# Five runs of attention products per pair of heads in place of seven, and maxima turned by an ordinary product

## The chip, the cores and the metric

The kernel runs on one core of a Trainium2 chip. The metric is the device time of one execution in microseconds (us). Three runs of the kernel before gave a median of 999.97 us (999.01 to 1001.33). The engines are named as the profile names them: PE is the matrix engine, PEld its loads of the stationary operand, DVE VectorE, ACT ScalarE, POOL GpSimd, SP SyncE, which issues nearly all DMAs.

## The reference

Two independent parts share one output of 2048 rows, 576 columns each.

```python
def _A_ref(x, wq, wk, wv, wo, beta):     # x: 1 x 2048 x 576, 32 heads of 18, 4 segments of 512 rows
    q, k, v = (heads and segments of) x @ wq, x @ wk, x @ wv
    phi = lambda t: jnp.where(t > 0, t + 1.0, jnp.exp(t))
    for s in range(4):
        logits = jnp.einsum("bhqd,bhkd->bhqk", qs, ks) * scale + mask      # causal inside the segment
        p = _softmax(logits, axis=-1)
        a_dot = jnp.einsum("bhqk,bhkd->bhqd", p, vs)
        a_mem = (phi(qs) @ M) / (phi(qs) @ z + 1e-6)
        o = g * a_mem + (1.0 - g) * a_dot
        M, z = M + phi(ks).T @ vs, z + sum(phi(ks))
    return concat(o) @ wo

def _B_ref(x, dft_seq_re, dft_seq_im, dft_hid_re, dft_hid_im):
    a = jnp.einsum("bsd,ed->bse", x, dft_hid_re)
    b = jnp.einsum("bsd,ed->bse", x, dft_hid_im)
    return jnp.einsum("ts,bse->bte", dft_seq_re, a) - jnp.einsum("ts,bse->bte", dft_seq_im, b)
```

The output holds A's result in columns 0 to 575 and B's in columns 576 to 1151.

## The kernel before

Float32 precision is kept by splitting operands into a high and a low part, so that a dense product of the reference is three products on PE (high by low, high by high, low by high).

**Stages.** Up to about 218 us the kernel projects q, k and v, builds the memory part, and writes q, k and v as split 16-bit pieces to DRAM. From there to about 930 us two streams of work share PE. The last 66 us are the product with `wo` (from L1013).

**The dense stream** is a generator `dense()`: all of part B. Per half (real, imaginary) it makes 16 tiles of `hidden` (L619, products in L628 to L633) and 16 tiles of `sequence` (L641, products through `product` in L583). Each of its products has a 128x128 stationary block and 288 moving columns, in f32r. Its results go to PSUM tiles `d`, of which there are three; they are freed by ACT (L634, L651) or by DVE (the subtractions of L635, shown at a line of the queue that runs late work, and of L653).

**The attention stream** is a generator `attention()` (L921). It goes through 68 periods `p`; 32 groups `G` of four heads make 64 pairs of heads, one of them even and one odd, and a pair's steps are spread over five periods (`F_LAG`, `T_LAG`, `V_LAG` = 2, 3, 4). All its products are on 16-bit operands. The scores of a head (512 queries by 512 keys, lower triangle) are made in three pieces, `ROWS`: kind 0 is row block 3 (one product of 512 columns), kind 1 row blocks 0 and 2 (products of 128 and 384), kind 2 row block 1 (256).

- `s_fill` (even head, L753): scores (L744) whose only use is the row minimum of their negative, which DVE takes (L750) into `NEGM`. The product's bank is free when the minimum is done.
- `f_fill` (odd head, L759): the same products and minima; then ACT takes the exponentials (`f_exp`, L773) from the same bank, `f_split_hi` and `f_split_lo` split the result, and `f_turn` transposes it by a DMA.
- `t_fill` (even head, L807): scores transposed (L818, L821, L826, L827), with the maxima coming in as extra rows of the product; ACT takes the exponentials (L830, L831).
- `pv` (L847): the products with v (L862, L863), many and short; `pv_out` (L865) normalizes on DVE.
- `maxima` (L791): POOL splits the minima of a group into three 16-bit pieces, in 24 columns of a 128x128 tile `MB`, zeros elsewhere. `maxima_transpose` (L799) turns that tile on PE against the identity, into columns 384 on of a bank, ACT copies 24 rows out (L803), and two DMAs put them beside the queries.

**Order of the work.** The schedule is written by hand. Each period has eight slots, and at each `yield` of `attention()` the main loop (L994 to L1001) adds as many dense products as make the two streams keep step by the costs in `SLOTS`. So the attention products of one slot, or of several where no dense products fall between them, form a run on PE, with dense products on both sides. Each engine works in program order. The operations that are put off with `later` are issued at the start of a later slot.

**PSUM banks** (`bank`, L564): the scores `s` alternate between two banks, the transposed scores `t` between two others, which kind 0 of `f_fill` shares; the second of a period's `t` banks also takes the turned maxima. One bank is for `pv`.

Of the kernel before, what the change touches and what calls it, by code (L numbers as in the profile page):

```python
# [15 lines left out]
BF16 = mybir.dt.bfloat16  # L16
# [24 lines left out]
def infini_attention_and_fnet(ctx: ExitStack, tc: tile.TileContext, xT, wqk, w8, wv, wo, beta, xtT, cT, hT, out):  # L41
    nc = tc.nc
    act, dve, pool, pe = nc.scalar, nc.vector, nc.gpsimd, nc.tensor
# [25 lines left out]
    ident16 = const.tile([P, P], BF16, name="ident16")  # L69
# [18 lines left out]
    def later(n, fn, *a):  # L88
        due.setdefault(clock[0] + n, []).append((fn, a))
# [112 lines left out]
    for i in range(2):  # L202
        kn.append(tuple(sk.tile([P, D], F32R, name=f"kn{n}{i}") for n in "hl"))
        t = sk.tile([P, 2, H, 19], F32R, name=f"vn{i}")
# [3 lines left out]
    for i in range(3):  # L208
        t = sb.tile([P, H, 55], BF16, name=f"vs{i}")
# [253 lines left out]
    def stacks(p_, i):  # L463
        qs_bufs.append(p_.tile([P, 4, L], BF16, name=f"qs{i}"))
        ks_bufs.append(p_.tile([P, 4, L], BF16, name=f"ks{i}"))
        pool.memset(ks_bufs[i].bitcast(F32)[96:], BF16_ONES)

    CAUSAL, NEGM, MB, OG = [], [], [], []
# [17 lines left out]

    def stack_load(G):
        if G < NG:
            s, g8 = divmod(G, 8)
            rows = slice(g8 * 72, g8 * 72 + 72)  # L490
            for n, (buf, src) in enumerate(((ks_bufs, kd), (qs_bufs, qd))):
                later(1 + n, dma, buf[G % 4][:NPAIR], src[s][rows].rearrange("(h d) c t -> (d c) h t", d=DH))

    def value_load(G):
        if G < NG:
            s, g8 = divmod(G, 8)
            VS[G] = sa.tile([P, 4, 220], BF16, name="vst", bufs=2)
            dma(VS[G], vd[s][:, :, g8])
# [65 lines left out]
    def bank(name, shape, dtype, tag):  # L564
        turns[tag] ^= 1
        return ps.tile(shape, dtype, name=name, tag=f"{tag}{turns[tag]}", bufs=1)
# [123 lines left out]
    def o_load(t):  # L690
        if t >= NT:
            return
        s, a = divmod(t, 4)
        o = O3[0].tile([P, 5, P], F32, name="o", bufs=3) if O3 else sb.tile([P, 5, P], F32, name="raw", tag="raw", bufs=3)
        dma(o[:, :4], od[s][:, a * P:a * P + P].rearrange("c p x -> p c x"))
        for i in range(2):
            dma(o[64 * i:64 * i + 64, 4], odt[s][64 * a:64 * a + 64])
        O[t] = o
# [92 lines left out]
    def maxima(G):  # L791
        m, b = NEGM[G % 2].rearrange("p (h n) -> p h n", h=2), MB[G % 2][:, :24].rearrange("p (h c n) -> p c h n", h=2, c=3)
        r = sa.tile([P, 2, 4], F32, name="negx", bufs=2)
        pool.tensor_copy(b[:, 0], m)
        pool.tensor_tensor(r, m, b[:, 0], OP.subtract)
        pool.tensor_copy(b[:, 1], r)
        pool.tensor_tensor(b[:, 2], r, b[:, 1], OP.subtract)

    def maxima_transpose(G, o):  # L799
        t = o[:, 384:448].bitcast(BF16)  # L800
        pe.transpose(t, MB[G % 2], ident16)
        w = sa.tile([24, P], BF16, name="mt", bufs=2)
        act.activation(w, t[:24], AF.Copy)  # L803
        for h in range(2):
            later(1, dma, qs_bufs[G % 4][NPAIR:NPAIR + 3, 2 * h].rearrange("c (n t) -> c n t", n=4), w[12 * h:12 * h + 12])
# [59 lines left out]
    def pv_out(n2):  # L865
        G, hh = divmod(n2, 2)
        s, g8 = divmod(G, 8)
        o = PV.pop(n2)
        og = OG[G % 2]
        h0 = 4 * g8 + 2 * hh  # L870
        w = o[:, 440:].rearrange("p (h i c) -> p h i c", h=2, c=1)
        b = o[:, :144].rearrange("p (h i d) -> p h i d", h=2, i=4)
        o = o[:, :440].rearrange("p (h i c) -> p h i c", h=2, i=4)
        a = sa.tile([P, 8, DH], F32, name="pa", bufs=2)
        dve.reciprocal(w, o[:, :, :, 54:])
        dve.tensor_tensor(w, w, g1[:, h0:h0 + 2, None, None].to_broadcast([P, 2, 4, 1]), OP.mult)
        dve.tensor_reduce(a, o[:, :, :, :54].rearrange("p h i (c d) -> p (h i) d c", c=3), axis=AX, op=OP.add)
        to = og[:, :, 36 * hh:36 * hh + 36].rearrange("p i (h d) -> p h i d", d=DH)
        a = a.rearrange("p (h i) d -> p h i d", h=2)
        if s == 0:  # L880
            dve.tensor_tensor(to, a, w.to_broadcast([P, 2, 4, DH]), OP.mult)
        else:
            dve.tensor_tensor(b, a, w.to_broadcast([P, 2, 4, DH]), OP.mult)
            dve.tensor_tensor(to, to, b, OP.add)
        if hh == 1:
            later(6, turn_out, G)
# [30 lines left out]
    F_LAG, T_LAG, V_LAG = 2, 3, 4  # L917
# [3 lines left out]
    def attention():  # L921
        for p in range(NP + V_LAG):
            def even(lag, fn, *a):
                if 0 <= p - lag < NP:
                    fn(2 * (p - lag), *a)

            def odd(lag, fn, *a):
                if 0 <= p - lag < NP:
                    fn(2 * (p - lag) + 1, *a)

            if p < 2:
                stacks(sa, p + 2)
                OG.append(sa.tile([P, 4, 72], F32, name=f"og{p}"))
            if p == 0:
                value_load(0)
                stack_load(1)
            if p % 2 == 0:
                later(39, value_load, p // 2 + 1)
                later(30, memory_load, p // 2)
            if p == NP + 1:  # L940
                o_load(0)
                o_load(1)
            even(T_LAG + 1, t_lo, 0)
            odd(F_LAG + 1, f_exp, 2)
            even(0, s_fill, 0)
            odd(F_LAG + 1, f_split_hi)
            yield SLOTS[0]
            G = p // 2 - 1 if p % 2 == 0 and 0 < p <= NP else None
            even(T_LAG, t_fill, 0)
            even(T_LAG, t_fill, 1, G)  # L950
            if G is not None and p < T_LAG:
                maxima_transpose(G, bank("trm", [P, L], F32, "t"))
            odd(F_LAG + 1, f_split_lo, pool, 512, 1280)
            yield SLOTS[1]
            even(0, s_fill, 1)
            odd(F_LAG + 1, f_split_lo, dve, 0, 512)
            yield SLOTS[2]
            even(V_LAG, pv)
            even(0, s_fill, 2)
            even(T_LAG, t_mask)  # L960
            yield SLOTS[3]
            odd(F_LAG, f_fill, 1)
            even(T_LAG, t_fill, 2)
            if p % 2 and p < NP:
                maxima(p // 2)
            yield SLOTS[4]
            odd(F_LAG + 1, f_turn)
            if p % 2:
                stack_load((p + 3) // 2)
                if p < 16:  # L970
                    later(2, copy_parts, 2, 8 + p // 2)
            elif 4 <= p < 36:
                later(2, copy_parts, 3, (p - 4) // 2)
            odd(F_LAG, f_fill, 0)
            even(T_LAG, t_hi)
            yield SLOTS[5]
            odd(V_LAG, pv)
            odd(F_LAG, f_fill, 2)
            odd(F_LAG, f_exp, 1)
            even(T_LAG, t_lo, 1)  # L980
            even(T_LAG, t_lo, 2)
            yield SLOTS[6]
            odd(F_LAG, f_exp, 0)
            if p >= V_LAG:
                pv_out(p - V_LAG)
            yield SLOTS[7]
# [7 lines left out]
    for w in attention():  # L994
        tick()
        ta += w
        while td / total_d < ta / total_a:
            t = next(d, BREAK)
            if t is BREAK:
                break  # L1000
            td += t  # L1001
# [11 lines left out]
    for t in range(NT):  # L1013
# [3 lines left out]
        for h in range(2):  # L1017
            cs = slice(h * 288, h * 288 + 288)
            o = ps.tile([P, 288], F32, name="d", bufs=3)
# [53 lines left out]
```

## Time and profile before

| | |
|---|---|
| median of three runs | 999.97 us |
| profiled execution | 998.12 us, of which the span is 996.4 us |
| granted clock of PE | 0.999 |
| busy share of the span: PE, PEld | 99%, 93% |
| DVE, ACT, POOL | 76%, 71%, 64% |
| products on PE | 9294 |

The busy time of PE is the union of its records, which are pipelined and overlap: a product of 288 columns has a record of about 0.3 us but follows the one before it after 0.13 us. So lengths of PE work are read as distances between starts. In the first dense record after a run of attention products the start stands close to that of the last attention product, though its columns come later; there the start of the second or third one is used. In the timeline a row stands for several like products that follow each other ("x2"), and its second figure is the length of all of them together.

### The profile page before, as it was taken

The page shows a single profiled execution, that of the slowest core. Times are in us where ns is not written, and L with a number is a line of the kernel's source. Part 1 is how long each engine was busy: PE and PEld are TensorE (multiplying, and loading weights), DVE is VectorE, ACT ScalarE, POOL GpSimd, SP SyncE. Part 2 cuts the span into 40 slices and gives each one's busy share as a digit, 9 for nine tenths or more (in the row PEclk, how much of TensorE's full clock was granted, in tenths as well). Part 3 has the DMA queues.
Part 4 walks back from the last instruction along what each step waited for, and adds up shares of the span by engine and source line. Part 5 has one row for each costly group of instructions (what it writes and reads, how often), then busy time and mean ns, then how long its engine had stood idle before and what let it go on. Part 6 is the DMA issues. An engine that isn't in the chain of part 4 may idle for free.

```text
span 996.4 us, 25591 instructions
## 1 busy us (share of the span) xinstructions
PE 988.1 (99%) x9294; PEld 923.0 (93%) x9294; DVE 753.6 (76%) x2052; ACT 712.3 (71%) x1680; POOL 634.8 (64%) x700
## 2 busy tenths in 40 slices
PE   9999999999999999999999999999999999999998
PEld 7989989899999999999999999999999999999998
DVE  6667668594678777878898888898889899998321
ACT  6757576663887877878788888877767777877243
POOL 2657576676767677766766777766767767767000
PEclk9999999999999999999999999999999999999999
DMA  7537456767688998899999987879998999989455
GB/s 239 197 117 254 177 178 238 239 232 228 154 185 213 208 252 222 209 235 222 251 226 243 213 206 203 178 198 225 234 222 222 231 237 248 243 189 192 136 151 139
DMA packets 305615, 208.92 MB, mean 210 GB/s; under 512 B 206289, under 2 KB 260433, under 8 KB 305489
## 3 DMA queue, kind: packets, MB, share of 16 engines
q1 hardware_dynamic: 305248, 207.15, 80.9%
q8 instruction: 73, 1.20, 0.5%
q14 instruction: 54, 0.43, 0.1%
q10 hardware_dynamic: 240, 0.14, 0.0%
HBM read 121.32 MB, written 57.93 MB: 180 GB/s over the span
## 4 chain that ended last, share of the span: by engine, by line
PE 86%; DVE 5%; ACT 4%; issue 2%; DMA 1%; POOL 1%; SPq 0%; POOLq 0%; DVEq 0%; ACTq 0%
PE d L583 39%; PE s L744 7%; PE d L84 6%; PE pv L862 4%; PE v L84 4%; PE qk L250 4%; PE d L628 3%; PE d L630 3%; PE d L629 3%; PE pv L863 2%; PE m L363 1%; PE t L818 1%; PE qk L84 1%; PE t L821 1%; DVE r L276 1%
## 5 line engine op out<-in xcount | busy, mean ns | idle before, releaser
L750 DVE CUSTOM_DVE_ANT_0 s<-s,causal 128x128 f32<-128x128 f32 (+3 forms) x512 | 249.8, 498 | 100.9 <-PE s L744 91.8
L456 POOL TENSOR_TENSOR clo<-craw,chi 128x512 fp32r<-128x512 f32 x158 | 216.3, 1369 | 95.4 <-ACT chi L451 69.4
L583 PE MATMUL d<-wide,chi 128*128 128x288 f32 x1408 | 266.3, 306 | 0.4 <-DVE y L653 0.4
L583 PEld LDWEIGHTS d<-wide,chi 128*128 128x128 f32 x1408 | 211.8, 189 | 2.4 <-DVE y L653 0.6
L583 PE MATMUL d<-wide,clo 128*128 128x288 f32 x704 | 177.6, 319 | 0.0
L784 POOL TENSOR_TENSOR hl<-pf,hl 128x768 f16<-128x768 f32 x64 | 112.8, 1763 | 70.1 <-ACT hl L780 56.8
L830 ACT ACTIVATE phi<-t 128x384 f16<-128x384 f32 x128 | 61.8, 482 | 103.0 <-PE t L827 102.9
L744 PE MATMUL s<-ks,qs 108*128 108x128 bf16 (+3 forms) x512 | 133.7, 304 | 1.7 <-DVE negm L750 1.2
L773 ACT ACTIVATE pf<-s,nb 128x128 f32<-128x128 f32 (+3 forms) x256 | 128.3, 527 | 6.2
L845 DVE TENSOR_TENSOR plo<-pf,phi 128x384 f16<-128x384 f32 (+1 forms) x128 | 126.3, 987 | 0.0
L583 PE MATMUL d<-ab,chi 128*128 128x288 f32 x640 | 125.9, 306 | 0.0
L583 PEld LDWEIGHTS d<-wide,clo 128*128 128x128 f32 x704 | 118.6, 189 | 1.6
L831 ACT ACTIVATE pf<-t 128x384 f32<-128x384 f32 (+1 forms) x192 | 99.5, 518 | 6.1 <-PE t L818 5.9
L451 ACT ACTIVATE chi<-craw 128x512 fp32r<-128x512 f32 x160 | 100.1, 626 | 3.7 <-PE d L583 1.4
L583 PEld LDWEIGHTS d<-ab,chi 128*128 128x128 f32 x640 | 98.5, 189 | 0.6
L780 ACT ACTIVATE hl<-pf 128x768 f16<-128x768 f32 (+1 forms) x128 | 87.4, 729 | 2.0
L583 PE MATMUL d<-ab,clo 128*128 128x288 f32 x320 | 84.8, 314 | 0.0
L628 PE MATMUL d<-wide,chi 128*128 128x288 f32 x256 | 84.0, 328 | 0.0
L630 PE MATMUL d<-wide,clo 128*128 128x288 f32 x256 | 75.6, 295 | 0.0
L629 PE MATMUL d<-wide,chi 128*128 128x288 f32 x256 | 75.6, 295 | 0.0
L784 DVE TENSOR_TENSOR hl<-pf,hl 128x512 f16<-128x512 f32 x64 | 67.7, 1058 | 0.1
L845 POOL TENSOR_TENSOR plo<-pf,phi 128x384 f16<-128x384 f32 x64 | 59.3, 927 | 12.9 <-ACT pf L831 10.3
(214 smaller groups left out, 2496.1 us busy)
## 6 DMA issues: line engine op xcount, KB each, us to landing
craw<-cT SPq DMA_DIRECT2D x128, 256.0 KB
ks<-kd SPq DMA_DIRECT2D x32, 432.0 KB
qs<-qd SPq DMA_DIRECT2D x32, 432.0 KB
craw<-xtT SPq DMA_DIRECT2D x32, 320.0 KB
vd<-vs SPq DMA_DIRECT2D x16, 440.0 KB
vst<-vd SPq DMA_DIRECT2D x32, 220.0 KB
qd<-p SPq DMA_DIRECT2D x16, 384.0 KB
kd<-p SPq DMA_DIRECT2D x16, 384.0 KB
```

The source lines that it names most:

```text
L84: pe.matmul(o, a, b, start=n == 0, stop=n == len(terms) - 1)
L451: act.activation(hi, raw[:, :4], AF.Copy)
L456: engine.tensor_tensor(lo, raw[:, :4], hi.bitcast(F32), OP.subtract)
L583: pe.matmul(o[h], a, b[:, h * 288:h * 288 + 288], start=start, stop=stop)
L628: pe.matmul(o, xh[:, k], wl[k][:, cs], start=k == 0, stop=False)
L629: pe.matmul(o, xh[:, k], wh[k][:, cs], start=False, stop=False)
L630: pe.matmul(o, xl[:, k], wh[k][:, cs], start=False, stop=False)
L744: pe.matmul(o[:, c:c + w], q[:, i * P:w], k[:, :w], start=True, stop=True)
L750: dve.tensor_tensor_reduce(o[:, c:c + w], o[:, c:c + w], CAUSAL[0][:, L - w:], scale=scale, scalar=-LOWEST, op0=OP.add, op1=OP.min, accum_ ...
L773: act.activation(f[:, FIRST_COL[i]:FIRST_COL[i] + w], o[:, c:c + w], AF.Exp, bias=nb[:, i:i + 1], scale=-1.0)
L784: engine.tensor_tensor(hl[:, 1, a:b], f[:, a:b], hl[:, 0, a:b], OP.subtract)
L845: (pool if kind == 2 else dve).tensor_tensor(lo[:, a:b], f[:, a:b], hi[:, a:b], OP.subtract)
```

## The change

Three edits. `s_fill` kind 0 of the even head moves from slot 0 to slot 1, ahead of `t_fill` kinds 0 and 1. `f_fill` kind 0 of the odd head moves from slot 5 to slot 4, behind `f_fill` kind 1 and `t_fill` kind 2. And `maxima_transpose` issues an ordinary product with the identity, which writes f32 to 128 columns, in place of a transpose, which writes 16-bit values to the same number of columns in half the space. The tile that is turned keeps its 128 columns.

```diff
     def maxima_transpose(G, o):
-        t = o[:, 384:448].bitcast(BF16)
-        pe.transpose(t, MB[G % 2], ident16)
+        t = o[:, 384:512]
+        pe.matmul(t, MB[G % 2], ident16, start=True, stop=True)
         w = sa.tile([24, P], BF16, name="mt", bufs=2)
         act.activation(w, t[:24], AF.Copy)
...
             even(T_LAG + 1, t_lo, 0)
             odd(F_LAG + 1, f_exp, 2)
-            even(0, s_fill, 0)
             odd(F_LAG + 1, f_split_hi)
             yield SLOTS[0]
             G = p // 2 - 1 if p % 2 == 0 and 0 < p <= NP else None
+            even(0, s_fill, 0)
             even(T_LAG, t_fill, 0)
             even(T_LAG, t_fill, 1, G)
...
             odd(F_LAG, f_fill, 1)
             even(T_LAG, t_fill, 2)
+            odd(F_LAG, f_fill, 0)
             if p % 2 and p < NP:
                 maxima(p // 2)
             yield SLOTS[4]
...
-            odd(F_LAG, f_fill, 0)
             even(T_LAG, t_hi)
             yield SLOTS[5]
```

## The prediction

> **What bounds the kernel now.** I read the page first, then the busy time of each engine in windows over the attention stage, then the waits of the matrix engine there, and last single stretches of the timeline. The first two rows are the page's, the other two the windows 308 to 586 and 653 to 930 us, which hold most of the stage that the change touches.
>
> ```profile
> span 996.4 us, 25591 instructions
> PE 988.1 (99%) x9294; PEld 923.0 (93%) x9294; DVE 753.6 (76%) x2052; ACT 712.3 (71%) x1680; POOL 634.8 (64%) x700
> ...
> core 0: us, PE busy (x) PEld busy (x) DVE busy (x) ACT busy (x) POOL busy (x), PEclk, DMA share, GB/s
> 308.00:586.00 278.00, 277.90 (x3012) 260.04 (x3010) 229.63 (x678) 222.74 (x530) 195.06 (x214) 1.00 0.94 227
> 653.00:930.00 277.00, 276.13 (x3006) 259.02 (x3005) 243.46 (x677) 205.81 (x476) 191.84 (x202) 1.00 0.94 220
> ```
>
> PE is busy for 277.90 of 278.00 us and 276.13 of 277.00 us, at a granted clock of 1.00; VectorE (DVE) has 12 to 17% to spare there. Records of PE overlap, so "busy" can also hide short waits; but no other engine is near its limit. So a nanosecond taken off PE's queue in this stage comes off the end, and one that other engines save does not. The waits of PE that the profile can show between 300 and 920 us are two groups:
>
> ```profile
> PE s L744 <- DVE negm L750: 0.4, 2, 0.2
> PE d L583 <- DVE y L653: 0.4, 1, 0.4
> ```
>
> Less than 1 us in all (waits too short to show under overlapping records come on top; three are below): there is little waiting to win, and any new wait is a loss.
>
> **The change part by part.** The dense products (f32r, 288 columns) alternate with runs of attention products (16 bit). `s_fill` of row block 3 (128x512, here s0) stood alone in slot 0 and now opens the run of slot 1; `f_fill` kind 0 (128x512, here f0) stood alone in slot 5 and now closes the run of slot 4. The orders of the two programs have the same 9294 products, and 429 runs of attention products against 315: 114 fewer. On DVE the matching minima move with them; the orders of ACT, POOL and SP, with their DMAs, are the same in both programs.
>
> *Fewer runs.* What a run costs beyond its own columns is seen in whole periods. Each row below is a window from the first `pv` product of one period to that of the next. I took only periods with the same 111 products (54 of them dense) and without a turning of maxima. By the timeline, the first has five runs (both lone products happened to fall next to others), the next two have six, the last two seven.
>
> ```profile
> 478.64:488.57 9.93, 9.93 (x111) 9.41 (x110) 7.60 (x26) 8.71 (x21) 8.79 (x11) 1.00 0.90 207
> 372.56:382.49 9.94, 9.94 (x111) 9.29 (x110) 7.76 (x26) 7.55 (x18) 6.03 (x7) 1.00 0.94 229
> 536.22:546.16 9.95, 9.95 (x111) 9.30 (x110) 7.29 (x25) 8.94 (x21) 6.76 (x7) 1.00 0.81 201
> 437.58:447.53 9.95, 9.95 (x111) 9.32 (x110) 8.54 (x24) 7.34 (x18) 6.74 (x9) 1.00 1.05 245
> 458.07:468.04 9.96, 9.96 (x111) 9.34 (x110) 8.45 (x29) 7.93 (x19) 6.37 (x10) 1.00 1.19 256
> ```
>
> 9.93, then 9.945, then 9.955 us on the mean: 25 ns for two runs, 12 to 13 ns each; with 5 ns of rounding on either end, 8 to 20 ns. I take 14 ns, a little above the means, since the five-run window is a single one. 114 x 14 ns = 1.6 us, with ends at 0.9 and 2.3 us. What the two forms look like in the timeline (start, length, line): a lone f0, and a run in which s0 already stands ahead of `t_fill` today.
>
> ```profile
> 507.55 0.39 PE L744 MATMUL s<-ks,qs 108*128 108x512 bf16 x1
> 507.59 0.62 PE L583 MATMUL d<-wide,clo 128*128 128x288 f32 x2
> 508.04 0.70 PE L583 MATMUL d<-wide,chi 128*128 128x288 f32 x4
> ...
> 687.50 0.39 PE L744 MATMUL s<-ks,qs 108*128 108x512 bf16 x1
> 687.72 0.39 PE L818 MATMUL t<-qs,ks 111*128 111x128 bf16 x4
> 687.95 0.33 PE L821 MATMUL t<-qs,ks 111*128 111x384 bf16 x1
> 688.11 0.22 PE L801 MATMUL t<-ident,mb 128*128 128x128 bf16 x1
> ```
>
> Inside a run s0 takes 0.22 us (687.50 to 687.72), which its 512 columns need anyway. Only the change between the two kinds is saved, so this is worth tens of nanoseconds a period.
>
> *Waits that leave with s0.* s0 needs the bank that the previous period's exponentials (L773) read. In three periods it came too early. The ACT row and the first pair of PE rows are one period; the others are the other two.
>
> ```profile
> 325.87 0.84 ACT L773 ACTIVATE pf<-s,nb 128x128 f32<-128x128 f32 x2
> ...
> 326.44 0.30 PE L583 MATMUL d<-ab,clo 128*128 128x288 f32 x1
> 326.76 0.38 PE L744 MATMUL s<-ks,qs 108*128 108x512 bf16 x1
> ...
> 521.11 0.29 PE L583 MATMUL d<-ab,clo 128*128 128x288 f32 x1
> 521.42 0.38 PE L744 MATMUL s<-ks,qs 108*128 108x512 bf16 x1
> ...
> 531.11 0.42 PE L583 MATMUL d<-wide,clo 128*128 128x288 f32 x2
> 531.37 0.70 PE L583 MATMUL d<-wide,chi 128*128 128x288 f32 x4
> 532.07 0.38 PE L744 MATMUL s<-ks,qs 108*128 108x512 bf16 x1
> ```
>
> The exponentials end at 326.71, and s0 starts at 326.76. From one dense product to the next run it took 0.32 and 0.31 us, and 0.70 us for four, where a dense product takes 0.13 to 0.14 (0.26 for two at 531.11, and the start of a run comes a little later): 0.18 + 0.17 + 0.16 = 0.5 us. In slot 1 s0 comes one stretch of dense products later, some 1 us or more, and the bank is free. What is late next in these periods is nothing that PE was not waiting for before. Ends: 0 (the wait comes back in another place) and 0.5; I take 0.5.
>
> *The turning of the maxima.* It stays 128 columns with the same stationary block and the same identity, and only loses the transpose flag and writes f32. Its row in the view of tile t (min/median/max ns), beside an ordinary product of 128 columns, and its place in one run:
>
> ```profile
> L818 PE MATMUL t<-qs,ks x256: 217/219/233, 252.6 to 913.7; 111*128 111x128 bf16 x128
> L801 PE MATMUL t<-ident,mb x31: 219/221/222, 262.5 to 894.6; 128*128 128x128 bf16 x31
> ...
> 512.65 0.40 PE L818 MATMUL t<-qs,ks 111*128 111x128 bf16 x4
> 513.05 0.22 PE L801 MATMUL t<-ident,mb 128*128 128x128 bf16 x1
> 513.08 0.52 PE L583 MATMUL d<-wide,clo 128*128 128x288 f32 x2
> 513.43 0.70 PE L583 MATMUL d<-wide,chi 128*128 128x288 f32 x4
> ...
> L583 PEld LDWEIGHTS d<-wide,chi 128*128 128x128 f32 x1408 | 211.8, 189 | 2.4 <-DVE y L653 0.6
> ```
>
> 221 against 219 ns: equal work. From its start to the third dense product it is 0.38 us, of which two dense products are 0.26: the turning takes about 0.11 us of PE, twice a 128-column product's own pace. I put the rest down to the next dense block's weight load (189 ns a record): a product this short cannot cover it, and the ordinary product will be as short. So zero. The ends are a loss of nothing (the rows are equal) and a gain of 1.6 us (second rival). ACT's copy of the 24 rows reads f32 instead of 16 bit; its result is wanted a period later, and ACT has a fifth of its time free here.
>
> The Trainium skill speaks against this part: "Perfetto Trace Analysis", section Transposes, says that a transpose should be issued as one and not as a standard matmul, because of logic that skips the arithmetic. It gives no price; by the two rows above there is none on PE.
>
> *The minima on DVE.* s0's minimum is now asked for later, f0's earlier and directly behind f1's. f0's can push a subtraction that frees a dense bank back by its own length; one such wait stands in the table above (L653, 0.4 us). I allow 0 to +1 us and take 0.
>
> **Sum.** 1.6 + 0.5 = 2.1 us. The profiled execution took 998.12 us (996.4 of span and 1.7 around it), 0.19% under the median of 999.97; it would come to 996.0 us. Against the median: 999.97 - 2.1 = 997.9 us. With the ends: 999.97 - 2.3 - 0.5 = 997.2, and 999.97 - 0.9 + 1.0 = 1000.1.
>
> **The rivals.**
>
> *Slower: s2 waits for s0's minimum.* s2, a slot or two behind, writes the bank that s0 used, so it needs s0's minimum to be over. Today's slack is already gone in some periods. The first three rows are such a period, the last three one with room.
>
> ```profile
> 668.64 1.21 DVE L845 TENSOR_TENSOR plo<-pf,phi 128x512 f16<-128x512 f32 x1
> 669.78 0.68 DVE L750 CUSTOM_DVE_ANT_0 s<-s,causal 128x512 f32<-128x512 f32 x1
> ...
> 670.57 0.27 PE L744 MATMUL s<-ks,qs 108*128 108x256 bf16 x1
> ...
> 359.49 0.69 DVE L750 CUSTOM_DVE_ANT_0 s<-s,causal 128x512 f32<-128x512 f32 x1
> 361.99 0.30 DVE L750 CUSTOM_DVE_ANT_0 s<-s,causal 128x128 f32<-128x128 f32 x1 [1.58 <-PE s L744]
> ...
> 362.19 0.27 PE L744 MATMUL s<-ks,qs 108*128 108x256 bf16 x1
> ```
>
> In the first, the minimum ends at 670.46 and s2 starts at 670.57. If s0's later start carried through to DVE, every tight period would stall PE by it: at 0.1 us a period over the 61 periods that have both `s_fill` and `t_fill`, 6.1 us, 999.97 - 2.1 + 6.1 = 1004 us. It decides from 2.1 us / 61 = 35 ns a period. Against it: in the tight period DVE is busy with older work until 669.78, later than s0 would come by any slot; where DVE is not behind, it idles 1.58 us before the next minimum, and s0's has 2 us until s2. Chance 0.14.
>
> *Faster: the ordinary product also closes the gap behind the turning.* A 128-column product takes 0.058 us inside a run (0.23 for L818's four, 687.72 to 687.95 above). If the other 0.055 us of the turning's 0.11 belongs to the transpose and not to the load, the 29 runs that end in it by the program's order save 29 x 0.055 = 1.6 us: 997.9 - 1.6 = 996.3 us. The rows' equal 219 and 221 ns speak against it. The Trainium skill, "TensorE: Matmul & The Clock Gate", Part 4, has 275 ns for a transpose in a kernel and a clock that doesn't rise for transposes; this trace has 221 ns and a clock of 1.00, so it doesn't agree. Chance 0.14.
>
> *The runs are not worth what the five windows say.* Periods also differ in DMA load and in where the runs fall; if the 25 ns were this, only the 0.5 us of waits remains, perhaps with one new wait as large: 999.5 to 1000. Chance 0.10.
>
> **How the numbers follow.** A measurement of this kernel can tell about 0.2%, 2.0 us, from no change. The forecast has chance 0.62 with its own range 996.4 to 999.4; its middle lies at 2.1 us, so I give 0.36 of it to faster and 0.26 to same. Faster: 0.36 + 0.14 = 0.50. Same: 0.26 + 0.10 = 0.36. Slower: 0.14. The range of 8 in 10 takes in the faster rival and the no-gain case, from 995.0 (the faster rival with the high end of the runs, and spread of the measurement) to 1000.8, and leaves the slower rival out.
>
> **What would show it.** Right: periods with the same products near 9.93 us, no lone 128x512 product of L744 in the timeline, the three gaps ahead of s0 gone, L801 at about 221 ns and still 0.11 us to the dense products behind it. Wrong: PE waits at L744 for L750 of more than 2 us, s2 starting right behind s0's minimum in many periods, or a gap behind L801 that is gone.

## The result, and the profile after

| | before | after |
|---|---|---|
| median | 998.98 us (12 runs, 997.21 to 1001.33) | 997.48 us (12 runs, 996.18 to 998.53) |
| ratio to before | | 0.9985, 95% interval 0.9978 to 0.9992 |
| profiled execution | 998.12 us, span 996.4 us | 997.94 us, span 996.2 us |

The changed kernel is faster by 0.15%, 1.5 us, with 0.8 to 2.2 us as the interval. That is inside the 0.2% named in the prediction as what a measurement can tell from no change, but the interval doesn't reach 1. The median of before over all twelve runs is 1.0 us below the 999.97 us of the first three, from which the forecast was counted; as a ratio the forecast was 0.9979 (2.1 us off), and 0.9985 was measured.

The page of the changed kernel first, then the second of the prediction's two large windows, then five periods. The columns of windows are: the stretch and its length, then busy time and instructions of PE, PEld, DVE, ACT and POOL, the granted clock, DMA share and GB/s.

```profile
span 996.2 us, 25590 instructions
PE 986.1 (99%) x9294; PEld 924.1 (93%) x9294; DVE 753.5 (76%) x2052; ACT 712.0 (71%) x1680; POOL 636.3 (64%) x700
...
653.00:930.00 277.00, 275.39 (x3003) 259.10 (x3003) 242.86 (x678) 205.08 (x475) 190.69 (x203) 1.00 0.92 220
...
479.00:488.92 9.91, 9.91 (x111) 9.38 (x110) 8.52 (x26) 8.68 (x21) 8.29 (x11) 1.00 1.05 213
373.17:383.09 9.92, 9.92 (x111) 9.33 (x110) 7.78 (x26) 7.54 (x18) 6.10 (x7) 1.00 0.91 222
536.11:546.03 9.92, 9.92 (x111) 9.33 (x110) 7.98 (x27) 9.12 (x22) 6.75 (x8) 1.00 0.87 199
438.04:447.98 9.94, 9.94 (x111) 9.35 (x110) 8.61 (x25) 7.32 (x18) 6.73 (x9) 1.00 1.06 248
458.51:468.43 9.92, 9.92 (x111) 9.34 (x110) 8.52 (x30) 7.93 (x19) 6.33 (x10) 1.00 1.17 233
```

PE is still the bound. The five windows are the same five periods, in the same order, as in the prediction. They took 9.93, 9.94, 9.95, 9.95 and 9.96 us there; now they take 9.91 (four runs) and 9.92, 9.92, 9.94, 9.92 (five runs each). In the large window from 653 to 930 us PE is busy for less than before, 275.39 against 276.13 us: it waits more there, although the kernel is faster. The waits of PE between 230 and 930 us say for what:

```profile
PE trm L801 <- POOL mb L797: 1.3, 1, 1.3
PE s L744 <- DVE negm L750: 1.2, 4, 0.4
```

Before there were two waits of L744 for L750, 0.4 us in all, and one of a dense product (L583) for a subtraction (L653), 0.4 us. Now there are four of the first kind, 1.2 us in all as far as overlapping records let them show, one long wait at the first turning of maxima, and none of a dense product in this view. The merged runs look as planned. The first is f0 (512 columns, 507.03) at the end of slot 4's run, the second s0 at the head of slot 1's, with the turning at its end:

```profile
506.93 0.27 PE L827 MATMUL t<-qs,ks 111*128 111x256 bf16 x1
507.03 0.38 PE L744 MATMUL s<-ks,qs 108*128 108x512 bf16 x1
507.06 0.62 PE L583 MATMUL d<-wide,clo 128*128 128x288 f32 x2
...
512.67 0.39 PE L744 MATMUL s<-ks,qs 108*128 108x512 bf16 x1
512.89 0.39 PE L818 MATMUL t<-qs,ks 111*128 111x128 bf16 x4
513.12 0.33 PE L821 MATMUL t<-qs,ks 111*128 111x384 bf16 x1
513.28 0.22 PE L801 MATMUL t<-ident,mb 128*128 128x128 bf16 x1
513.31 0.51 PE L583 MATMUL d<-wide,clo 128*128 128x288 f32 x2
513.66 0.70 PE L583 MATMUL d<-wide,chi 128*128 128x288 f32 x4
...
L801 PE MATMUL t<-ident,mb x31: 219/221/222, 263.6 to 894.5; 128*128 128x128 bf16 x31
```

The turning lasts 221 ns as before, and from its start to the third dense product it is still 0.38 us (513.28 to 513.66).

### The profile page after: what moved, and what is told of

It reads as the page before. It is cut to its first block, busy times and chain, and to the rows that moved or that the text cites. A ratio compares the mean times of both kernels' runs of the same rounds, so it can differ in the third digit from the quotient of the medians.

```text
span 996.2 us, 25590 instructions
## 1 busy us (share of the span) xinstructions
PE 986.1 (99%) x9294; PEld 924.1 (93%) x9294; DVE 753.5 (76%) x2052; ACT 712.0 (71%) x1680; POOL 636.3 (64%) x700
## 4 chain that ended last, share of the span: by engine, by line
PE 84%; DVE 6%; ACT 5%; issue 2%; DMA 2%; POOL 1%; SPq 0%; POOLq 0%; DVEq 0%; ACTq 0%
PE d L583 38%; PE s L744 7%; PE d L84 6%; PE v L84 4%; PE pv L862 4%; PE qk L250 4%; PE d L628 3%; PE d L629 3%; PE d L630 3%; PE pv L863 2%; PE m L363 1%; PE t L818 1%; PE qk L84 1%; DVE r L276 1%; PE t L821 1%
## 5 line engine op out<-in xcount | busy, mean ns | idle before, releaser
L750 DVE CUSTOM_DVE_ANT_0 s<-s,causal 128x128 f32<-128x128 f32 (+3 forms) x512 | 248.1, 504 | 94.0 <-PE s L744 84.8
L583 PE MATMUL d<-wide,chi 128*128 128x288 f32 x1408 | 261.7, 303 | 0.0
L583 PEld LDWEIGHTS d<-wide,chi 128*128 128x128 f32 x1408 | 210.7, 188 | 2.7 <-issue 1.1
L583 PE MATMUL d<-wide,clo 128*128 128x288 f32 x704 | 173.3, 313 | 0.0
L744 PE MATMUL s<-ks,qs 108*128 108x128 bf16 (+3 forms) x512 | 132.8, 303 | 2.7 <-DVE negm L750 2.1
L583 PE MATMUL d<-ab,chi 128*128 128x288 f32 x640 | 123.3, 302 | 0.0
L845 DVE TENSOR_TENSOR plo<-pf,phi 128x384 f16<-128x384 f32 (+1 forms) x128 | 122.9, 960 | 0.0
L583 PEld LDWEIGHTS d<-wide,clo 128*128 128x128 f32 x704 | 117.8, 189 | 1.9 <-issue 0.5
L583 PEld LDWEIGHTS d<-ab,chi 128*128 128x128 f32 x640 | 97.8, 189 | 0.5
L583 PE MATMUL d<-ab,clo 128*128 128x288 f32 x320 | 83.0, 308 | 0.0
L628 PE MATMUL d<-wide,chi 128*128 128x288 f32 x256 | 81.3, 318 | 0.0
L629 PE MATMUL d<-wide,chi 128*128 128x288 f32 x256 | 75.7, 296 | 0.0
L630 PE MATMUL d<-wide,clo 128*128 128x288 f32 x256 | 75.6, 295 | 0.0
L845 POOL TENSOR_TENSOR plo<-pf,phi 128x384 f16<-128x384 f32 x64 | 61.4, 959 | 13.8 <-ACT pf L831 13.3
```

The lines of the kernel that those rows point to most:

```text
L583: pe.matmul(o[h], a, b[:, h * 288:h * 288 + 288], start=start, stop=stop)
L628: pe.matmul(o, xh[:, k], wl[k][:, cs], start=k == 0, stop=False)
L629: pe.matmul(o, xh[:, k], wh[k][:, cs], start=False, stop=False)
L630: pe.matmul(o, xl[:, k], wh[k][:, cs], start=False, stop=False)
L744: pe.matmul(o[:, c:c + w], q[:, i * P:w], k[:, :w], start=True, stop=True)
L750: dve.tensor_tensor_reduce(o[:, c:c + w], o[:, c:c + w], CAUSAL[0][:, L - w:], scale=scale, scalar=-LOWEST, op0=OP.add, op1=OP.min, accum_ ...
```

## The experiments

The rivals I set against each other were these: the time comes from the runs alone (theory of the prediction); the ordinary product contributes too; the moves bring a new wait on DVE that takes part of it back. Times are medians, ratios are against the kernel before run beside them (medians of 998.81, 999.22 and 998.87 us in the three sets).

**1. Both moves, the transpose kept.**

```diff
     def maxima_transpose(G, o):
-        t = o[:, 384:512]
-        pe.matmul(t, MB[G % 2], ident16, start=True, stop=True)
+        t = o[:, 384:448].bitcast(BF16)
+        pe.transpose(t, MB[G % 2], ident16)
```

> Both moves, but the maxima still turned by a transpose. If the time came from fewer runs of attention products (315 in place of 429) and the turning is worth nothing, this is as fast as the whole change: 1 to 2 us under the kernel before (ratio 0.998 to 0.999). If the ordinary product brought it (29 runs end in the turning, 0.055 us each), this is at the kernel before within 0.5 us, ratio 0.9995 to 1.0005.

Measured: 998.18 us, ratio 0.9988 (0.9976 to 1.0000). That agrees with the whole change (0.9985), but the interval also reaches into the rival's range, 0.9995 and up; experiment 2 and the table at the end of this section decide.

**2. The ordinary product alone**, in the order of before (429 runs): the same edit the other way round.

> The ordinary product alone, the slots as before: 429 runs. If a product of 128 columns can't cover the next dense block's weight load whatever its kind, the time is that of the kernel before (within 0.5 us) and the gap behind L801 stays 0.11 us to the dense products. If the gap belongs to the transpose, the run is 1.6 us faster and the gap falls to about 0.06 us.

Measured: 998.96 us, ratio 1.0006 (0.9997 to 1.0016). By its interval the product brings at most 0.3 us. The gap behind it is what it was behind the transpose, 0.38 us from its start to the third dense product (timeline of this kernel, the run of the same period):

```profile
512.99 0.22 PE L801 MATMUL t<-ident,mb 128*128 128x128 bf16 x1
...
513.37 0.69 PE L583 MATMUL d<-wide,chi 128*128 128x288 f32 x4
```

**3. The whole change, with the turning ahead of the run's last wide product**, so that 384 columns stand between it and the dense products.

```diff
+            if maxima_of is not None:
+                maxima_turn(maxima_of, o)          # the product of maxima_transpose alone
             (product of 384 columns)
             if maxima_of is not None:
-                maxima_transpose(maxima_of, o)
+                maxima_copy(maxima_of, o)          # its copy and its two DMAs
```

> The whole change, with the turning placed ahead of the 384-column product of the same bank, so that runs end in 384 columns and not in 128. If the 0.055 us behind the turning is an uncovered weight load, some 29 runs lose it: 1.6 us less than the whole change, some 3 us (0.3%) under the kernel before. If it is the price of the turning itself, nothing changes against the whole change. The turning also waits for its maxima 0.16 us sooner, which could give some of it back.

Measured: 996.33 us, ratio 0.9979 (0.9970 to 0.9987). The run of the same period, to be held against the 512.67 one above:

```profile
512.12 0.39 PE L744 MATMUL s<-ks,qs 108*128 108x512 bf16 x1
512.34 0.39 PE L825 MATMUL t<-qs,ks 111*128 111x128 bf16 x4
512.57 0.22 PE L801 MATMUL t<-ident,mb 128*128 128x128 bf16 x1
512.63 0.33 PE L830 MATMUL t<-qs,ks 111*128 111x384 bf16 x1
512.65 0.57 PE L583 MATMUL d<-wide,clo 128*128 128x288 f32 x2
513.06 0.69 PE L583 MATMUL d<-wide,chi 128*128 128x288 f32 x4
```

From s0 to the third dense product it is 0.94 us here (512.12 to 513.06) and 0.99 us in the changed kernel (512.67 to 513.66), for the same products. So in this run 0.05 us belongs to the place of the 128-column product at the end, since the product itself is unchanged; 29 of them would make 1.5 us, and against the moves alone (0.9988) 0.9 us were measured, in overlapping intervals.

**4. Two more runs per period**: before, with a few dense products put between kinds 0 and 1 of `t_fill`, and between `f_fill` 1 and `t_fill` 2 (538 runs for 429).

```diff
             even(T_LAG, t_fill, 0)
+            if T_LAG <= p < NP:
+                yield None
             even(T_LAG, t_fill, 1, G)
...
             odd(F_LAG, f_fill, 1)
+            if T_LAG <= p < NP:
+                yield None
             even(T_LAG, t_fill, 2)
...
+        if w is None:                              # main loop: dense products up to the next break
+            t = next(d, BREAK)
+            td += (next(d, BREAK) if t is BREAK else t) or 0.0
+            continue
```

> The kernel before with two more runs a period: one dense step between the t products of kind 0 and kind 1, and one between f kind 1 and t kind 2; 538 runs in place of 429. The first cut leaves 61 runs that end in an ordinary product of 128 columns. If a change of kind costs 14 ns and an uncovered load 0.055 us after any 128-column product: 109 x 14 ns + 61 x 55 ns = 1.5 + 3.4 = 4.9 us slower (0.5%). If only a transpose leaves the gap: 1.5 us slower. If runs cost nothing (the gain was in the waits of s0): no change.

Measured: 1003.18 us, ratio 1.0047 (1.0035 to 1.0060), 4.4 us more than before. The new cuts behind 128-column products pay the same gap as the turning:

```profile
484.43 0.40 PE L818 MATMUL t<-qs,ks 111*128 111x128 bf16 x4
484.64 0.77 PE L583 MATMUL d<-ab,chi 128*128 128x288 f32 x4
485.25 0.34 PE L821 MATMUL t<-qs,ks 111*128 111x384 bf16 x1
```

Four products of 0.058 us and four dense ones of 0.133 us need 0.76 us; from 484.43 to 485.25 it is 0.82. I fitted all runs between 230 and 925 us in this way: time from a run's first product to that of the next, less 133 ns for each dense product and the columns of the others. For a run that ends in a wide product 13 ns are left here (13 before, 14 in the changed kernel; 10 to 13 in the three if the price of a column is fitted too); one that ends in a 128-column product of L818 has 60 ns on top, one that ends in the turning 58. Times the counts: 109 x 13 ns = 1.4 us, and 61 x 60 ns = 3.7 us, 5.1 us for the 4.4 (3.5 to 6.0) measured. So the time bears out the two prices together. It doesn't show the price of a run by itself: the gaps' 3.7 us alone lie in the interval too, and the 13 ns rest on the fit and on experiment 6 (in the table below).

**5 and 6. One move alone**, each with the transpose: s0's move alone (373 runs), f0's move alone (371 runs). The edits are against the changed kernel; that of the transpose is as in experiment 1.

```diff
 s0 alone:                                   f0 alone:
-            odd(F_LAG, f_fill, 0)   slot 4  -            even(0, s_fill, 0)      slot 1
+            odd(F_LAG, f_fill, 0)   slot 5  +            even(0, s_fill, 0)      slot 0
```

> Of the whole change only the move of s0 (slot 0 to slot 1): 373 runs. Theory, from the two profiles: 56 fewer runs (0.8 us) and three waits of s0 gone (0.5 us) against new waits of s2, because s0's minimum now stands behind whatever DVE work falls between slots 0 and 1 (y subtractions L653, weight splits L124): about +1.5 us, and a wait at the first turning near 240 us of about 1 us. Net 0, ratio 0.999 to 1.001, with the long waits of s2 near 669, 813, 854 and 886 us in its profile. Rival: the waits of s2 come from the earlier f0; then this is 1.3 us faster and shows none of them.

> Only the move of f0 (slot 5 to slot 4): 371 runs, s0 alone as before. Theory: 58 x 14 ns = 0.8 us faster and no new waits: ratio 0.999. The s2 waits stay those of the kernel before, the three waits of s0 stay. Rival: f0's minimum ahead of other DVE work makes the new waits; then it is 0.5 to 1 us slower than the kernel before.

Measured: s0 alone 998.19 us, ratio 0.9999 (0.9987 to 1.0011); f0 alone 998.05 us, ratio 0.9994 (0.9982 to 1.0005). Neither can be told from 1 by the time. The waits of PE between 300 and 930 us tell them apart; the first row is s0 alone, the others f0 alone:

```profile
PE s L744 <- DVE negm L750: 1.3, 4, 0.4
...
PE d L583 <- DVE y L653: 0.4, 1, 0.4
PE s L744 <- DVE negm L750: 0.3, 2, 0.2
```

f0's move leaves the waits of before. s0's move brings the four waits of the changed kernel, and takes away the one of a dense product for L653. Where they come from is seen in one of them, in the changed kernel (DVE and PE):

```profile
851.43 1.25 DVE L845 TENSOR_TENSOR plo<-pf,phi 128x512 f16<-128x512 f32 x1
852.61 2.21 DVE L124 TENSOR_TENSOR wide<-raw,wide 128x576 fp32r<-128x576 f32 x1
854.74 0.69 DVE L750 CUSTOM_DVE_ANT_0 s<-s,causal 128x512 f32<-128x512 f32 x1
855.04 0.18 PE L863 MATMUL pv<-vst,plo 128*128 128x37 bf16 x1
855.54 0.27 PE L744 MATMUL s<-ks,qs 108*128 108x256 bf16 x1 [0.32 <-DVE negm L750]
```

and at the same place before:

```profile
852.34 1.33 DVE L845 TENSOR_TENSOR plo<-pf,phi 128x512 f16<-128x512 f32 x1
853.59 0.69 DVE L750 CUSTOM_DVE_ANT_0 s<-s,causal 128x512 f32<-128x512 f32 x1
854.20 1.60 DVE L124 TENSOR_TENSOR wide<-raw,wide 128x576 fp32r<-128x576 f32 x1
...
856.07 0.27 PE L744 MATMUL s<-ks,qs 108*128 108x256 bf16 x1
```

Here DVE takes its work in the order of the program. Before, s0's minimum was issued in slot 0, ahead of whatever the dense stream put on DVE between slots 0 and 1. Now that work (here a split, L124, of 2.21 us; in the three other places a subtraction, L653, of 0.44 us) stands ahead of s0's minimum, and s2 on PE waits until the minimum is over. The same order has a good side, near 741 us: there a subtraction that stands ahead of s0's minimum frees a dense bank sooner, and the wait of the dense product is gone (in the kernel before it is 0.4 us in the view of waits).

**7. Experiment 3 with that work held back**: what the dense stream gives to DVE in L653 and L124 between slots 0 and 1 is issued only after s0's minimum, or earlier where the next product of `sequence` begins before that.

```diff
-                dve.tensor_tensor(y[:, cs], y[:, cs], o, OP.subtract)       # L653
+                hold(dve.tensor_tensor, y[:, cs], y[:, cs], o, OP.subtract) # kept in a list while HOLD
-            later(wait, low)                                                # L124
+            later(wait, hold, low)
...
+            HOLD[0] = p < NP
             yield SLOTS[0]
             G = p // 2 - 1 if p % 2 == 0 and 0 < p <= NP else None
             even(0, s_fill, 0)
+            release()
...
     def product(steps, count, evacuate):
+        if HELD:
+            release()
```

> The version with the early turning, and DVE's y subtractions (L653) and weight splits (L124) that fall between slots 0 and 1 held back until s0's products are issued, so that s0's minimum is ahead of them. Theory: the waits of s2 near 668, 812, 853 and 885 us (0.62, 0.28, 0.52 and 0.62 us in the profile with the early turning) go, 1.5 to 2 us less than that version: about 4 us under the kernel before, ratio 0.996. Rival: the held subtractions free the dense banks later, and PE waits there instead: no gain or a loss.

Measured: 995.60 us, ratio 0.9969 (0.9958 to 0.9981). Against the early turning 1.5 to 2 us less were expected; experiment 8, which is that kernel with a transpose and ran in the same set, is only 0.7 us above. In the trace the order of before is back, and s2 comes without the wait; the last two rows are all the waits of PE between 300 and 930 us:

```profile
850.25 1.21 DVE L869 TENSOR_TENSOR plo<-pf,phi 128x512 f16<-128x512 f32 x1
851.39 0.69 DVE L765 CUSTOM_DVE_ANT_0 s<-s,causal 128x512 f32<-128x512 f32 x1
852.00 1.60 DVE L137 TENSOR_TENSOR wide<-raw,wide 128x576 fp32r<-128x576 f32 x1
853.80 0.27 PE L759 MATMUL s<-ks,qs 108*128 108x256 bf16 x1
...
PE d L598 <- DVE y L102: 0.4, 1, 0.4
PE s L759 <- DVE negm L765: 0.2, 1, 0.2
```

(L869, L765, L137, L759 and L598 are the L845, L750, L124, L744 and L583 of the changed kernel; L102 issues what was held back. Experiment 3 had 1.1 us in three waits of L744, and none of a dense product.) So the trace shows the cause of the waits of s2. It shows the rival too, at one place: near 740 us a held subtraction frees its dense bank late, and PE waits as it did in the kernel before near 742 us. By distances of starts the waits of s2 lose 1.5 us and this one costs 0.7 us, which is why less was won than expected. By the ratios alone nothing is settled, for their intervals overlap with those of the next kernel; the table below has 0.8 us for the holding back.

**8. Experiment 3 with the transpose in place of the product.**

> The early turning with both moves, but by a transpose. If the kind of product is worth nothing anywhere, this is as fast as the early turning with the ordinary product (ratio to before 0.997 to 0.9987). If the transpose has a price inside a run (the five runs of the kernel before that had it there say at most 10 ns each), it is at most 0.3 us slower.

Measured: 996.26 us, ratio 0.9972 (0.9960 to 0.9983), as experiment 3 (0.9970 to 0.9987). No difference by the kind of product is to be seen in this place either.

**9 to 11. The wait at the first turning.** In the profile of the changed kernel the first turning, at 241 us, waits 1.3 us for POOL; in that of before it doesn't. Three kernels went into one set: the changed kernel once more, the changed kernel with that first turning two slots later, and experiment 7 with the same.

```diff
             even(T_LAG, t_fill, 0)
             even(T_LAG, t_fill, 1, G)
-            if G is not None and p < T_LAG:                  # slot 1
-                maxima_transpose(G, bank("trm", [P, L], F32, "t"))
...
             even(0, s_fill, 2)
+            if G is not None and p < T_LAG:                  # slot 3
+                maxima_transpose(G, bank("trm", [P, L], F32, "t"))
```

> The whole change once more, for a second profile and a second time. If the wait at the first turning (near 240 us, behind a load of craw that landed 2 us later than in the kernel before) belongs to this program, it is there again, 0.9 to 1.5 us; if it was chance, it is gone and the span is about 1 us shorter. Time: 1 to 2 us under the kernel before, ratio 0.998 to 0.999.

> The whole change with the very first turning (period 2 alone) moved from slot 1 to slot 3, some 3 us later, where its input is ready. If the wait at 240 us also falls on executions without a profile, this is about 1 us (0.1%) faster than the whole change; if the dense stream just waits for the late load a little later, nothing is gained.

> The held version with the same late first turning: the best of what is known. 4 us under the kernel before (ratio 0.996) if the 240 us wait is real in every execution, 3 us (0.997) if it is not.

Measured: the changed kernel again 997.31 us, ratio 0.9984 (0.9972 to 0.9996), with a span of 994.7 us in its profile; with the later turning 997.19 us, 0.9980 (0.9971 to 0.9988); experiment 7 with the later turning 995.35 us, 0.9962 (0.9950 to 0.9974), span 993.2 us. The rows down to the first turning at 241.46 are the changed kernel's first profile, the last two its second one:

```profile
237.74 0.63 ACT L451 ACTIVATE chi<-craw 128x512 fp32r<-128x512 f32 x1 [3.10 <-DMA craw<-xtT]
...
241.21 0.20 POOL L797 TENSOR_TENSOR mb<-negx,mb 128x8 bf16<-128x8 f32 x1
241.46 0.23 PE L801 MATMUL trm<-ident,mb 128*128 128x128 bf16 x1 [1.31 <-POOL mb L797]
...
236.08 0.63 ACT L451 ACTIVATE chi<-craw 128x512 fp32r<-128x512 f32 x1 [1.50 <-DMA craw<-xtT]
239.94 0.22 PE L801 MATMUL trm<-ident,mb 128*128 128x128 bf16 x1
```

The same program has the wait in one execution and not in the other: a load for the dense stream (`craw`) landed later, ACT and POOL were late behind it, and with POOL the maxima. So the change alone doesn't bring the wait, and the 1.5 us between the spans of the two profiles of one program (996.2 and 994.7) is as large as the change. Putting the turning later brought 0.3 us or nothing, not the 1 us or so that the first profile seemed to promise; but in that set the load came late in none of the three profiles, so there may have been no wait to save. It stays open why the load came late in seven of the ten profiles of kernels with a move, and in none of the three without one (before and experiments 2 and 4). Experiment 11 is the fastest version found: its median is 3.5 us below before's in the same set.

**All runs in one stretch.** Whole times also hold what happens ahead of the attention stage, such as that late load. From the start of the first `pv` product to the start of the last one (near 267 and 928 us) every kernel has the same 7139 products. One profile of each program, and two of the changed kernel, give:

| kernel | runs in the whole program | us |
|---|---|---|
| before | 429 | 661.40 |
| 2, product alone | 429 | 661.62 |
| the change; 9, once more; 1, moves alone | 315 | 660.21; 660.20; 660.22 |
| 10, first turning later | 315 | 660.34 |
| 5, s0's move alone | 373 | 660.93 |
| 6, f0's move alone | 371 | 660.66 |
| 3 and 8, turning ahead of the wide product | 315 | 659.13; 659.07 |
| 7 and 11, DVE work held back | 315 | 658.30; 658.54 |
| 4, more runs | 538 | 665.30 |

Kernels whose order in this stretch is the same agree within 0.24 us, though the spans of two profiles of one program differ by 1.5. So the change is worth 1.2 us here, f0's move 0.7 and s0's 0.5; the ordinary product brings nothing; the turning's place is worth 1.1 us, 0.04 us for each of 29; and the added runs cost 3.9 us. f0's move leaves the waits of PE as they were, and 56 runs fewer in this stretch save 0.74 us: 13 ns each, from the traces of two kernels and without a fit.

## Why the prediction was right, and where it was off

*Fewer runs: right.* 114 runs at 14 ns were forecast, 1.6 us. The fit of all runs gives 13.2 ns before and 13.7 ns in the changed kernel, experiment 6 has 13 ns, and the periods moved by 10 to 40 ns for the one to two runs they lost: 114 x 13.5 ns = 1.5 us. The lower and upper end were 8 and 20 ns; the rounding that the prediction names makes the upper one 18, which changes nothing here.

*Waits that leave with s0: right.* The three waits (0.5 us) are not in the traces of the changed kernel, and stand in those of experiments 2, 4 and 6, where s0 wasn't moved.

*The turning: right, at zero.* 221 ns before and after, 0.38 us to the third dense product before and after, 660.22 against 660.21 us in the table's stretch with and without the transpose; experiment 2's interval (0.9997 to 1.0016) leaves a gain of at most 0.3 us, so the rival of 1.6 us is out. The 0.055 us of the gap that the prediction put down to the short product do belong to it: experiment 3 removes most of them by order alone, experiment 4 shows the same 60 ns behind an ordinary product, and behind the `pv` products of 37 columns the fit has 84 ns in the changed kernel (three runs end so). That it is the next weight load which a short product can't cover is my reading; no run changes the load alone. The Trainium skill fits that reading, "TensorE: Matmul & The Clock Gate", section LDWEIGHTS: it has a load of P columns last P/1.2 ns, 107 ns for 128 columns, which would by estimate leave 107 - 58 = 49 ns behind 128 columns, where 58 to 60 were measured, and 107 - 25 = 82 ns behind a `pv` product, where the fit has 84; the records of the load, 189 ns each in the prediction's row, don't show the 107 directly. Its rule against transposing by a standard matmul ("Perfetto Trace Analysis", section Transposes) shows no price here: experiments 1 and 2 leave none, and 3 and 8 differ by less than their intervals.

*The minima on DVE: the step that was mis-sized.* The prediction allowed 0 to +1 us, took 0, and looked for the danger in f0's minimum; +1.5 us came, from s0's. By the timeline of PE, s2 starts 0.55, 0.35, 0.50 and 0.55 us after the last `pv` product at four places of the changed kernel (669, 813, 855 and 887 us; 855.04 to 855.54 is shown above), where `pv` products follow each other at 0.025 us: 1.85 us of waiting. Before there were two such places, with 0.19 us each, 0.33 us of waiting: +1.5 us. (The view of waits counts only what no overlapping record covers, hence its 1.2 us.) The mechanism is that of the slower rival, s2 waiting for s0's minimum, at 4 periods and not at 61. The argument against the rival, that in the tight period DVE is busy until 669.78 whatever s0 does, looked only at when PE makes s0. The minimum was moved in DVE's order too, behind a subtraction of the dense stream, in that very period:

```profile
668.19 1.21 DVE L845 TENSOR_TENSOR plo<-pf,phi 128x512 f16<-128x512 f32 x1
669.32 0.44 DVE L653 TENSOR_TENSOR y<-y,d 128x288 f32<-128x288 f32 x1
669.69 0.69 DVE L750 CUSTOM_DVE_ANT_0 s<-s,causal 128x512 f32<-128x512 f32 x1
...
670.48 0.27 PE L744 MATMUL s<-ks,qs 108*128 108x256 bf16 x1 [0.38 <-DVE negm L750]
```

DVE and PE both come to this place 0.45 us earlier than before (668.19 for 668.64 on DVE, and as much for the last `pv` product). The subtraction uses that up on DVE: s0's minimum starts at 669.69 for 669.78, and s2 at 670.48 for 670.57, so that PE waits some 0.36 us longer.

*The sum: close in part by luck.* -1.5 for the runs, -0.5 for the waits of s0 and +1.5 for the waits of s2 make -0.5 us. In the table's stretch the change is worth -1.2 us, and -1.5 us (-0.8 to -2.2) was measured for the whole. Of the 0.7 us between -0.5 and -1.2, 0.3 us are shorter waits for the dense banks: the one near 742 us is gone, because a subtraction now stands ahead of s0's minimum, and a smaller one near 758 us is new. The other 0.4 us stay open; by the table they belong rather to s0's move, since f0's 0.74 us are its 56 runs at 13 ns. So the forecast of -2.1 us lacked a loss of 1.5 us and gains of 0.7 us, and it was luck that the second made up for half of the first. With its DVE term at the +1.5 us that the traces show for s2, its own sum would have been -0.6 us.

## What to carry to other kernels

When a product is moved, follow what its result makes other engines do: the consumer moves in its own engine's queue too, and the work that slips in ahead of it there is what the next product waits for; the work that it slips ahead of may be awaited as well, so that both waits have to be counted. A change between 16-bit and f32r runs costs 13 to 14 ns in this kernel, so that merging runs is worth little; ending a run in a wide product instead of a 128-column one is worth 0.04 to 0.05 us each time, for nothing but an order. Where the effect is 1 to 2 us, profile the same program twice before a wait is put down to an edit, and compare the stretch between two instructions that both programs have.

## What the runs showed of the hardware

- A run's last product sets a gap ahead of the f32r products: 58 to 60 ns behind 128 columns, transpose or not (fit of all runs), 84 ns behind 37 columns; behind 384 or 512 only the 13 to 14 ns of any run are left.
- One form on DVE, the 128x512 subtraction of L845, took 1.21 to 1.33 us in the places shown here, and from 0.68 to 2.18 us over the kernel before; the split of L124 that is shown took 1.60 us before and 2.21 us in the changed kernel. What makes it so was not tested.
- One program's profiled span was 996.2 us and 994.7 us in two executions at nearly the same clock (0.999 and 1.00), though the stretch of 7139 products in it took 660.21 and 660.20 us; one late load was the start of a 1.3 us wait of PE in the first.
